# Loading the first batch's Q and K pairs straight into the buffers that TensorE transposes

## The chip, the core and the metric

The kernel runs on one core of one Trainium2 chip. A core has four engines that compute: TensorE (PE in the profile; its weight loads are listed apart, as PEld), VectorE (DVE), ScalarE (ACT) and GpSimd (POOL). SyncE (SP) only issues transfers. Each engine works through its own list of instructions in order, and waits on semaphores for what it needs from the others. Transfers between device memory and the on-chip SBUF go through 16 DMA engines; POOL, SP and ACT can each issue them, and each issuer has a queue of its own. TensorE writes to PSUM, which VectorE and ScalarE read.

The metric is the device time of one execution in microseconds (us), as a median of several runs.

## What is computed

Windowed attention for 8 batches and 8 heads over 576 positions of 64 channels, and behind it a feed-forward layer with squared ReLU on all 4,608 tokens:

```python
# q, k, v: (8, 8, 576, 64) float32
scores = scale * q @ k.transpose(0, 1, 3, 2)           # scale = 1/8
mask = abs(pos[:, None] - pos[None, :]) <= 32
attn = softmax(where(mask, scores, -1e9))
x = (attn @ v).transpose(0, 2, 1, 3).reshape(4608, 512)
h = x @ w_in                                           # (512, 2048)
g = maximum(h, 0) ** 2
out = g @ w_out                                        # (2048, 512), float32
```

## The kernel before

Every batch is cut into three groups of 192 positions; group G is number G mod 3 of batch G div 3, so there are 24 groups. The work of a group, with the names used below and the lines of the profile:

- **Loads** of q, k and v, cast to bfloat16 on the way (POOL). For batches 0 and 1 q and k come as *pairs* (`load_pair`, L426): one partition holds two neighbouring positions of each head, so a written piece is 128 numbers, in the order head, position of the pair, channel. A VectorE copy (L429) then regroups this staging buffer (`PR`, NPR of them for each of q and k) into the buffer `RAW`: all first positions, then all second positions. Group 0 of batch 0 takes another way (`load_hw`, L407): SP loads it in float32, and VectorE and ScalarE cast it into `RAW` (L414, L417). v is loaded in two blocks a group (`load_v`, L443), and VectorE copies the 64 rows that two groups share (`copy_v`, L450).
- **Turn** (`turn_pe`, L485), for batches 0 and 1: TensorE transposes `RAW` in 8 pieces of 128 columns, through the identity matrix, into PSUM; ScalarE (q, L513) or VectorE (k, L516) copies the result to `QT` or `KT`. Later batches are transposed by DMAs that SP issues (L524).
- **S**, the scores (`scores`, L565): two blocks of 8 matmuls, called S1A and S1B for group 1. ScalarE takes the exponential (L589), VectorE multiplies by the mask (L594); for group 0 the mask is added by TensorE ahead of the scores (L548).
- **P** (`pv`, L613 and L622): P0A and P0B for group 0, attention times v. VectorE then takes the reciprocal of the row sums (L641) and normalizes into `xa` or `xb` (L644).
- **T** (`xturn`): the normalized rows are transposed into `XT`, on TensorE for groups 0 to 2 (L666, L671, L696, L701), by DMA later.

The feed-forward layer runs over tokens. **A** is the first product (`mm1`, L737): "A0.12" is tokens from 0 and columns 12 and 13 of the 16 blocks of 128 columns of `w_in`; while a step has 192 tokens, one such item is 8 matmuls. ScalarE applies the ReLU (L743), VectorE squares (L746). **B** is the second product (`mm2`, L757): "B0.2" is the third quarter of the 2,048 terms for output block 0, 4 matmuls.

The weights come in quarters, each one load on POOL's queue: quarter i of `w_in` (L456) is needed first by A0.(4i), and quarter i of `w_out` (L461) by B0.i. In what follows w_in 0 to 3 and w_out 0 to 3 are these quarters.

The order of the work is not written out by hand. Each operation is recorded with its engine, its estimated duration and a key; the method `schedule` plays the program forward with these estimates (those of transfers among them) and gives each engine its fixed list. `OPENING` names the loads at the start in the order of their keys. Where the plan leaves TensorE idle at the start, the program puts in matmuls on a buffer of zeros (L322, "fillers") that compute nothing.

The order of the first loads on POOL's queue is: k1, w_in 0, v0.0, v1.1, q1, v0.1, q2, k2, v1.0, w_in 1, w_in 2, w_in 3, v2.0, v2.1, w_out 1, k3, v3.0, q3, q5, w_out 0, w_out 2, k4, and so on. Here q2 is the load of q for group 2, and v1.0 is block 0 of v for group 1. The sizes written are 192 KB for a pair load of 96 partitions (224 KB for k3, 160 KB for k2 and k5), 512 KB for a weight quarter, and 64 to 128 KB for a block of v.

Of the kernel before, what the change touches and what calls it, by code (L numbers as in the profile page):

```python
# [18 lines left out]
RING = 1536  # L19
NV, NRAW = 6, 6  # L20
NTURN = 2
NXT = 3
LEAD = 13.0
LAG = 9.0
# [9 lines left out]
PMOVE = 20  # L34
# [11 lines left out]
PQ = 100  # L46
VCS = 6
NDUP = 1
NPR = 3
LSLACK1 = 1000  # L50
HOLD = {}
KMIN = 0.5
HOLDT = 26000
KSPL = 0
# [1 line left out]
NSPLIT = 3  # L56
HWB = 150
HWQ = {'k': 'SP', 'q': 'SP'}
HWC = {"k": ("DVE", "ACT"), "q": ("ACT", "DVE")}
NPAIR = 6  # L60
FIRST = {}
T512 = 2048
NBIAS = 1
PKEY = 0.2
MKEY = (-9.5, -6.5)
VSET = (-9.8, -6.8)
ESPLIT = 0
IOTA = -1
OPENING = [("k", 1), ("w1", 0), ("v", 0, 0), ("v", 1, 1), ("q", 1), ("v", 0, 1), ("q", 2), ("k", 2), ("v", 1, 0), ("w1", 1),
           ("w1", 2), ("w1", 3), ("q", 5), ("v", 2, 0), ("v", 2, 1), ("w2", 1), ("k", 3), ("v", 3, 0), ("q", 3), ("w2", 0), ("w2",  # L70
           2), ("k", 4), ("v", 3, 1), ("q", 4), ("v", 5, 0), ("v", 5, 1), ("w2", 3), ("hq", 0), ("k", 5), ("v", 4, 0), ("v", 4, 1),
           ("hk", 0)]
WARM = 40000
LAST = ((0, 256), (256, 384), (384, 512))
KC = ((0, 224), (224, 192), (416, 160))
# [7 lines left out]
class Prog:  # L83
# [43 lines left out]
    def schedule(self):  # L127
# [53 lines left out]
        while True:  # L181
# [21 lines left out]
            first = pool[e][0]  # L203
            soon = min((w[0] for w in wait[e] if t < HOLDT and w[0] <= t + HOLD.get(e, 0) and w[2].key < first[0] - KMIN), default=None)
            if soon is not None and soon - t < first[2].dur:
# [66 lines left out]
def act(n):  # L272
    return 175 + 0.833 * n


def dve(n, fast=True):
    return 153 + (0.52 if fast else 1.04) * n


class Gen:  # L280
# [5 lines left out]
    def alloc(self):  # L286
# [111 lines left out]
    def load_hw(self, t, g, key):  # L398

        t0, n = KC[g] if t == "k" else (192 * g, 192)  # L400
        h = n // 2
        raw = self.RAW[t][g % NRAW]
        u = 2 * (t == "q")
        f = self.OEB[:, u:u + 2, :].rearrange("p a c -> p (a c)")
        s = (self.q if t == "q" else self.k)[0][:, t0:t0 + n, :].rearrange("h (p r) d -> p h (r d)", r=2)
        oe = [("oe", u), ("oe", u + 1)]
        self.p.rec(HWQ[t], lambda e: e.dma_start(f[0:h, :].rearrange("p (h c) -> p h c", c=128), s), writes=oe,  # L407
                   dma=(f"h{u}", g), key=key, dur=420, move=(h // 2, HMOVE), name=f"h{t}{g}")
        for r in range(2):
            x = f[0:h, :].rearrange("p (h r d) -> p h r d", r=2, d=64)[:, :, r, :]  # L410
            y = raw[0:h, r, :].rearrange("p (h d) -> p h d", d=64)
            w = [("raw", t, g % NRAW, r)]
            if HWC[t][r] == "ACT":
                self.p.rec("ACT", lambda e, x=x, y=y: e.activation(y, x, ACTF.Copy), reads=oe, writes=w, key=key, dur=600,  # L414
                           name=f"c{t}{g}{r}")
            else:
                self.p.rec("DVE", lambda e, x=x, y=y: e.tensor_copy(y, x), reads=oe, writes=w, key=key, dur=430, name=f"c{t}{g}{r}")  # L417

    def load_pair(self, t, b, g, key):

        t0, n = KC[g] if t == "k" else (192 * g, 192)
        h = n // 2
        G = 3 * b + g
        pr, raw = self.PR[t][G % NPR], self.RAW[t][G % NRAW]
        s = (self.q if t == "q" else self.k)[b][:, t0:t0 + n, :].rearrange("h (p r) d -> p h (r d)", r=2)
        self.p.rec("POOL", lambda e: e.dma_start(pr[0:h, :].rearrange("p (h c) -> p h c", c=128), s), writes=[("pr", t, G % NPR)],  # L426
                   dma=(f"{t}p{G % NPR}", G), key=key, dur=500 + 3 * h, move=(h // 2, PMOVE), name=f"{t}{b}{g}",
                   slack=LSLACK1 if b else 0)
        self.p.rec("DVE", lambda e: e.tensor_copy(raw[0:h, :, :].rearrange("p r (h d) -> p r h d", d=64),  # L429
                                                  pr[0:h, :].rearrange("p (h r d) -> p r h d", r=2, d=64)),  # L430
                   reads=[("pr", t, G % NPR)], writes=[("raw", t, G % NRAW, x) for x in range(2)], key=3 * G - LEAD - PKEY if b == 0 else key, dur=430,
                   name=f"c{t}{b}{g}")
# [39 lines left out]
    def turn_pe(self, t, b, g, key):  # L472
        dst, n = self.turned(t, b, g)
        h, G = n // 2, 3 * b + g
        raw = self.RAW[t][G % NRAW]
        if b:
            bank, tag = (self.AT[:, 512:1024], self.half(1)) if t == "q" else (self.AT[:, 0:512], self.half(0))
        else:
            bank, tag = (self.OUTP[0][:], ["outp0"]) if t == "k" else (self.HT[1][:], ["ht1"])
        ps = bank.bitcast(BF16)  # L480

        def f(e):
            for j in range(4):
                for x in range(2):
                    mm = e.transpose(ps[:, n * j + h * x:n * j + h * x + h], raw[0:h, x, 128 * j:128 * j + 128],  # L485
                                     self.ID[0:h, 0:h])
            return mm

        self.p.rec("PE", f, reads=[("raw", t, G % NRAW, 0), ("raw", t, G % NRAW, 1), "id"], writes=tag, key=key,
                   dur=8 * 52, name=f"turn{t}{b}{g}")  # L490
        if G < NPAIR:
            src = ps[:, 0:4 * n].rearrange("p (j r q) -> p j r q", j=4, r=2)
            dq = dst.rearrange("p j (q r) -> p j q r", r=2)
            dst = dst.rearrange("p j (q r) -> p j r q", r=2)
            if G < ESPLIT:
                self.p.rec("DVE", lambda e: e.tensor_copy(dst[:, 0:2], src[:, 0:2]), reads=tag, writes=[(t + "h", b % 2, g)],
                           key=key, dur=dve(2 * n, False), name=f"ev{t}{b}{g}h")
                self.p.rec("ACT", lambda e: e.activation(dst[:, 2:4], src[:, 2:4], ACTF.Copy), reads=tag,
                           writes=[(t + "t", b % 2, g)], key=key, dur=act(2 * n), name=f"ev{t}{b}{g}t")
                return  # L500
            dn = dve(4 * n, False)
        else:
            src = ps[:, 0:4 * n].rearrange("p (j q) -> p j q", j=4)
            dn = dve(4 * n)
        w = (t + "t", b % 2, g)
        if t == "k" and G == 0 and KSPL:
            for x, (c0, c1) in enumerate(((0, KSPL), (KSPL, h))):
                self.p.rec("DVE", lambda e, c0=c0, c1=c1: e.tensor_copy(dq[:, :, c0:c1, :].rearrange("p j q r -> p j r q"),
                                                                        src[:, :, :, c0:c1]), reads=tag,
                           writes=[("kt0", x)] if x == 0 else [w], key=key, dur=dve(8 * (c1 - c0), False), name=f"ev{t}{b}{g}{x}")  # L510
            return
        if t == "q":
            self.p.rec("ACT", lambda e: e.activation(dst, src, ACTF.Copy), reads=tag, writes=[w], key=key,  # L513
                       dur=act(4 * n), name=f"ev{t}{b}{g}")
        else:
            self.p.rec("DVE", lambda e: e.tensor_copy(dst, src), reads=tag, writes=[w], key=key, dur=dn,  # L516
                       name=f"ev{t}{b}{g}")
# [16 lines left out]
    def scores(self, G, ws):  # L534
# [35 lines left out]
        if G == 0 and KSPL:  # L570
            rd = [("qt", i, g), ("kt0", 0)] + [("kt", i, 0)] * (1 in ws)
        two = lambda x: b >= NTURN or 3 * b + x < ESPLIT
        rd += [("qh", i, g)] * two(g) + [("kh", i, x) for x in range(max(g - 1, 0), g + 1) if two(x)]
# [78 lines left out]
    def xturn(self, G):  # L652
# [146 lines left out]
    def build(self):  # L799
# [79 lines left out]
    def opening(self):  # L879
        return OPENING  # L880

# [31 lines left out]
```

## Time and profile before

| | |
|---|---|
| median of 3 runs (lowest to highest) | 302.2 us (301.95 to 302.28) |
| the profiled execution | 301.87 us, of which the instructions span 299.9 us |
| PE busy | 291.9 us, 97% of the span |
| VectorE, ScalarE, POOL busy | 167.2, 160.3 and 107.1 us |
| POOL's DMA queue | 106,016 packets, 17.93 MB |

The table is of one profiled execution; its time stands 1.97 us above its span, for what lies around the first and the last instruction. Starts in the trace are microseconds from the start of the span. In a timeline row the columns are: start, time from the first start to the last end, engine, line, operation, what is written and read, sizes, and how many instructions are merged; in brackets stands the idle time of the engine before the row, and what ended it. Matmuls overlap, so the cost of one group on TensorE is the distance from its start to the start of the next one and not the second column.

### The profile page before, as it was taken

The numbers are of one execution on the slowest core, as the hardware profiler recorded it, in microseconds if no ns is written. First come the engines' busy times: TensorE is split into PE (matmuls) and PEld (weight loads), VectorE is DVE, ScalarE is ACT, GpSimd is POOL, SyncE is SP. The second block draws the span as 40 slices with busy tenths as digits, with TensorE's granted clock in tenths as the row PEclk, the third lists the DMA queues.
The fourth block names the chain that finished last, engine by engine and source line by source line (L and its number), as shares of the span: only waits on it lengthen the run. The fifth ranks groups of instructions, "written<-read, shape, count | busy, mean of one in ns | idle before, by whom it ended". The sixth has DMA issues, their size and how long they took to land.

```text
span 299.9 us, 6209 instructions
## 1 busy us (share of the span) xinstructions
PE 291.9 (97%) x2394; PEld 171.8 (57%) x2431; DVE 167.2 (56%) x385; ACT 160.3 (53%) x250; POOL 107.1 (36%) x143
## 2 busy tenths in 40 slices
PE   7899999999999999999999999999999999999996
PEld 3578866848677767664544454444544444444445
DVE  6898775737674767563656666665666632222100
ACT  3497834836467656750765476536744643443312
POOL 8993336503544354455256335533500000000000
PEclk9999999999999999999999999999999999999999
DMA  9999999997999999999999999999992120100112
GB/s 169 176 206 184 196 177 174 169 176 137 164 169 165 95 162 146 155 138 186 180 168 131 114 166 156 125 149 156 154 128 70 55 61 35 37 35 35 38 70 105
DMA packets 160636, 39.83 MB, mean 133 GB/s; under 512 B 149984, under 2 KB 156128, under 8 KB 160608
## 3 DMA queue, kind: packets, MB, share of 16 engines
q0 software_dynamic: 106016, 17.93, 89.3%
q1 hardware_dynamic: 49264, 12.14, 28.5%
q10 hardware_dynamic: 5328, 9.37, 9.1%
q8 instruction: 19, 0.31, 0.5%
q14 instruction: 9, 0.07, 0.1%
HBM read 36.70 MB, written 9.44 MB: 154 GB/s over the span
## 4 chain that ended last, share of the span: by engine, by line
PE 90%; DMA 5%; POOL 3%; issue 1%; ACT 0%; POOLq 0%; ACTq 0%
PE ht L737 41%; PE outp L757 40%; DMA w<-in_moe_w_in_dram 5%; PE at L622 4%; PE at L565 4%; POOL v L443 1%; POOL w L456 1%; PE at L485 1%; PE ht L782 1%; PE outp L782 1%; POOL kpair L426 1%; POOL qpair L426 1%; ACT rt L743 0%; ACT oe L792 0%; POOL dif L325 0%
## 5 line engine op out<-in xcount | busy, mean ns | idle before, releaser
L737 PE MATMUL ht<-xt,w 128*128 128x256 bf16 (+2 forms) x885 | 140.0, 302 | 1.3 <-DMA w<-in_moe_w_in_dram 0.5
L757 PE MATMUL outp<-w,gt 128*128 128x512 bf16 x536 | 133.0, 379 | 1.3
L743 ACT ACTIVATE rt<-ht 128x512 bf16<-128x512 f32 (+1 forms) x152 | 85.9, 578 | 87.1 <-PE ht L737 85.1
L737 PEld LDWEIGHTS ht<-xt,w 128*128 128x128 bf16 x896 | 81.3, 98 | 43.8 <-ACT rt L743 0.6
L746 DVE TENSOR_TENSOR gt<-rt 128x512 bf16<-128x512 bf16 (+1 forms) x152 | 61.5, 408 | 61.6 <-ACT rt L743 60.0
L757 PEld LDWEIGHTS outp<-w,gt 128*128 128x128 bf16 x560 | 51.9, 98 | 54.1 <-ACT oe L767 1.0
L394 POOL DMA_DIRECT2D kraw<-in_k_dram x36 | 27.7, 778 | 107.3 <-PE at L622 56.8
L589 ACT ACTIVATE e<-at 128x1024 bf16<-128x1024 f32 x46 | 44.8, 1021 | 8.7 <-PE at L565 8.4
L594 DVE TENSOR_TENSOR pt<-e,mask 128x1024 bf16<-128x1024 bf16 x46 | 31.8, 691 | 29.0 <-ACT e L589 28.9
L443 POOL DMA_DIRECT2D v<-in_v_dram x48 | 38.2, 809 | 0.0
L767 ACT ACTIVATE oe<-outp 128x512 f32<-128x512 f32 x35 | 21.1, 604 | 29.6 <-PE outp L757 29.6
L394 POOL DMA_DIRECT2D qraw<-in_q_dram x36 | 27.7, 778 | 0.0
L622 PEld LDWEIGHTS at<-v,pt 128*128 128x128 bf16 x384 | 18.3, 98 | 9.9 <-DMA v<-in_v_dram 0.6
L622 PE MATMUL at<-v,pt 128*128 128x65 bf16 x384 | 20.1, 194 | 0.5 <-ACT pt L586 0.5
L644 DVE TENSOR_TENSOR xa<-at,rs 64x512 bf16<-64x512 f32 x24 | 16.7, 695 | 0.9
L644 DVE TENSOR_TENSOR xb<-at,rs 128x512 bf16<-128x512 f32 x24 | 16.5, 689 | 0.7
L565 PEld LDWEIGHTS at<-qt,kt 64*128 64x128 bf16 x384 | 10.8, 94 | 8.7 <-issue 7.1
L565 PE MATMUL at<-qt,kt 64*128 64x128 bf16 x384 | 15.2, 217 | 0.2
L641 DVE RECIPROCAL rs<-at 64x8 f32<-64x8 f32 (+1 forms) x48 | 10.0, 209 | 9.1 <-PE at L622 7.7
L650 DVE MEMSET at<- 64x520 f32 x23 | 11.3, 492 | 3.5 <-DVE xa L644 2.6
L450 DVE COPY v<-v 64x512 bf16<-64x512 bf16 x16 | 5.9, 372 | 5.1 <-PE ht L737 2.9
L789 DVE COPY oe<-ht 128x128 f32<-128x128 f32 x1 | 0.3, 292 | 14.5 <-PE ht L782 14.5
(67 smaller groups left out, 83.2 us busy)
## 6 DMA issues: line engine op xcount, KB each, us to landing
out_dram<-oe ACTq DMA_DIRECT2D x35, 256.0 KB, 3.2
qraw<-in_q_dram POOLq DMA_DIRECT2D x36, 96.0 KB, 5.8
w<-in_moe_w_in_dram POOLq DMA_DIRECT2D x4, 512.0 KB, 10.7
v<-in_v_dram POOLq DMA_DIRECT2D x16, 128.0 KB, 6.6
w<-in_moe_w_out_dram POOLq DMA_DIRECT2D x4, 512.0 KB, 18.8
v<-in_v_dram POOLq DMA_DIRECT2D x16, 96.0 KB, 7.0
kraw<-in_k_dram POOLq DMA_DIRECT2D x12, 112.0 KB, 4.6
kraw<-in_k_dram POOLq DMA_DIRECT2D x12, 96.0 KB, 4.9
```

Source lines behind the costliest of these rows:

```text
L394: self.p.rec("POOL", lambda e, j=j: e.dma_start(raw[0:h, j, :].rearrange("p (h d) -> p h d", h=8), s[:, j]), writes=[("raw", t, G % NRAW, ...
L443: self.p.rec("POOL", lambda e, j=j, lo=lo, hi=hi, k0=k0: e.dma_start(vt[lo - k0:hi - k0, j, :, 0:64], self.v[b, :, lo:hi, :].rearrange("h ...
L565: mm = e.matmul(sc[:, 512 * par + 128 * j:512 * par + 128 * j + 128], kt[r:r + 64, j, k0:k0 + 128], q, start=G >= NBIAS, stop=True, skip_g ...
L589: self.p.rec("ACT", lambda e, e_=e_, sc=sc: e.activation(e_[:], sc, ACTF.Exp, scale=0.125), reads=tags[w], writes=[("e", n % 2)], key=key, ...
L594: self.p.rec("DVE", lambda e, pt=pt, ee=ee, mb=mb: e.tensor_tensor(pt[:], ee, mb, ALU.mult), reads=[("e", n % 2), ("mask", mi)], writes=[( ...
L622: mm = e.matmul(avp[:, c:c + 65], pt[:, 4 * (h % 2) + h // 2, :], vt[:, w, h, 0:65], start=(w == 0 and y == 0), stop=True, skip_group_chec ...
L644: self.p.rec("DVE", lambda e: e.tensor_tensor(x[r0:128, :].rearrange("p (x y c) -> p x y c", x=2, y=4), av[:, :, :, 0:64], rb, ALU.mult), ...
L737: mm = e.matmul(ht[:, n * x:n * x + n], self.W1[:, ft, 128 * d:128 * d + 128], self.XT[:, ft, r:r + n], start=(ft == 0), stop=(ft == 3))
L743: self.p.rec("ACT", lambda e: e.activation(rt[:, 0:c], ht[:, 0:c], ACTF.Relu), reads=[f"ht{k % 2}"], writes=[("rt", k % 4)], key=key, dur= ...
L746: self.p.rec("DVE", lambda e: e.tensor_tensor(gt[:, d0:d0 + len(ds), r:r + n], rr, rr, ALU.mult), reads=[("rt", k % 4)], writes=[("gt", s, ...
L757: mm = e.matmul(op[:], gt[:, d, r:r + 128], self.W2[:, d, :], start=(d == 0), stop=(d == 15))
L767: self.p.rec("ACT", lambda e: e.activation(oe, op[:], ACTF.Copy), reads=[f"outp{u % 2}"], writes=[("oe", u % 4)], key=key, dur=act(512), n ...
```

## The change

Loads of pairs for groups 1 and 2 of batch 0 go straight into `RAW`, in the pair order, and the regrouping copy falls away; the staging buffers are used from group 3 on. The two casts of group 0 write the same pair order. The turn of groups 0 to 2 then takes 64 columns at a time, and sends the two heads of a pair of heads to the lower and the upper 64 partitions of PSUM, so that the result in PSUM is what it was: 16 transposes instead of 8. Some settings of the planner change with it, and the first loads are ordered anew.

```diff
+NRAWP = 3
+TCOL = 200
...
-NPR = 3
+NPR = 4
...
-HOLD = {}
+HOLD = {'PE': 300}
...
-VSET = (-9.8, -6.8)
+VSET = (-12, -9)
...
-OPENING = [("k", 1), ("w1", 0), ("v", 0, 0), ("v", 1, 1), ("q", 1), ("v", 0, 1), ("q", 2), ("k", 2), ("v", 1, 0), ("w1", 1),
...
+OPENING = [("q", 2), ("v", 0, 1), ("v", 0, 0), ("k", 1), ("v", 1, 0), ("q", 1), ("w1", 0), ("hq", 0), ("k", 2), ("w1", 1), ("v",
+           1, 1), ("w1", 2), ("w1", 3), ("v", 2, 0), ("v", 2, 1), ("w2", 0), ("q", 3), ("hk", 0), ("k", 4), ("k", 3), ("v", 5, 0),
+           ("w2", 1), ("v", 4, 1), ("w2", 2), ("v", 3, 0), ("q", 4), ("v", 4, 0), ("v", 3, 1), ("w2", 3), ("v", 5, 1), ("k", 5),
+           ("q", 5)]
...
-            y = raw[0:h, r, :].rearrange("p (h d) -> p h d", d=64)
+            y = self.pairs(raw)[0:h].rearrange("p (h r d) -> p h r d", r=2, d=64)[:, :, r, :]
...
+    def pairs(self, raw):
+        return raw[:].rearrange("p a c -> p (a c)")
+
...
+        if G < NRAWP:
+            self.p.rec("POOL", lambda e: e.dma_start(self.pairs(raw)[0:h].rearrange("p (h c) -> p h c", c=128), s),
+                       writes=[("raw", t, G % NRAW, x) for x in range(2)], dma=(f"{t}P{G}", G), key=key, dur=500 + 3 * h,
+                       move=(h // 2, PMOVE), name=f"{t}{b}{g}")
+            return
...
-                    mm = e.transpose(ps[:, n * j + h * x:n * j + h * x + h], raw[0:h, x, 128 * j:128 * j + 128],
-                                     self.ID[0:h, 0:h])
+                    c = n * j + h * x
+                    if G < NRAWP:
+                        for u in range(2):
+                            d = 256 * j + 128 * u + 64 * x
+                            mm = e.transpose(ps[64 * u:64 * u + 64, c:c + h], self.pairs(raw)[0:h, d:d + 64], self.ID[0:h, 0:h])
+                        continue
+                    mm = e.transpose(ps[:, c:c + h], raw[0:h, x, 128 * j:128 * j + 128], self.ID[0:h, 0:h])
...
-                   dur=8 * 52, name=f"turn{t}{b}{g}")
+                   dur=8 * 52 + TCOL * (G < NRAWP), name=f"turn{t}{b}{g}")
```

In `OPENING`, "w1" is w_in, "w2" is w_out, and "hq" and "hk" are the loads of group 0. `TCOL` is the planner's estimate in ns of what the 16 pieces add to a turn. `HOLD` lets the planner keep an engine waiting up to 300 ns for an operation with a lower key. `VSET` moves two small settings of v's buffers on VectorE. `NPR` is the number of staging buffers.

The order on POOL's queue becomes: q2, v0.1, v0.0, k1, v1.0, q1, w_in 0, k2, w_in 1, v1.1, w_in 2, w_in 3, v2.0, v2.1, w_out 0, q3, k4, k3, v5.0, w_out 1, v4.1, w_out 2, v3.0, q4, v4.0, v3.1, w_out 3, v5.1, k5, q5. The two loads on SP's queue stay first there.

More of the change, by code (lines that the diff above doesn't have):

```diff
@@ L58 @@
 HWQ = {'k': 'SP', 'q': 'SP'}
-HWC = {"k": ("DVE", "ACT"), "q": ("ACT", "DVE")}
+HWC = {'k': ('DVE', 'ACT'), 'q': ('ACT', 'DVE')}
 NPAIR = 6
@@ L65 @@
 MKEY = (-9.5, -6.5)
-VSET = (-9.8, -6.8)
+VSET = (-12, -9)
 ESPLIT = 0
 IOTA = -1
-OPENING = [("k", 1), ("w1", 0), ("v", 0, 0), ("v", 1, 1), ("q", 1), ("v", 0, 1), ("q", 2), ("k", 2), ("v", 1, 0), ("w1", 1),
-           ("w1", 2), ("w1", 3), ("q", 5), ("v", 2, 0), ("v", 2, 1), ("w2", 1), ("k", 3), ("v", 3, 0), ("q", 3), ("w2", 0), ("w2",
-           2), ("k", 4), ("v", 3, 1), ("q", 4), ("v", 5, 0), ("v", 5, 1), ("w2", 3), ("hq", 0), ("k", 5), ("v", 4, 0), ("v", 4, 1),
-           ("hk", 0)]
+OPENING = [("q", 2), ("v", 0, 1), ("v", 0, 0), ("k", 1), ("v", 1, 0), ("q", 1), ("w1", 0), ("hq", 0), ("k", 2), ("w1", 1), ("v",
+           1, 1), ("w1", 2), ("w1", 3), ("v", 2, 0), ("v", 2, 1), ("w2", 0), ("q", 3), ("hk", 0), ("k", 4), ("k", 3), ("v", 5, 0),
+           ("w2", 1), ("v", 4, 1), ("w2", 2), ("v", 3, 0), ("q", 4), ("v", 4, 0), ("v", 3, 1), ("w2", 3), ("v", 5, 1), ("k", 5),
+           ("q", 5)]
 WARM = 40000
```

## The prediction

> **What bounds the kernel now.** I read the page first, then TensorE's waits, then the chain of waits and the first 41 us of the timeline.
>
> ```profile
> span 299.9 us, 6209 instructions
> PE 291.9 (97%) x2394; PEld 171.8 (57%) x2431; DVE 167.2 (56%) x385; ACT 160.3 (53%) x250; POOL 107.1 (36%) x143
> ```
>
> TensorE is busy for 97% of the span, so time can only come from what it waits for, or from fillers at the start, which count as busy. TensorE's waits from 24.2 us (by its matmuls) to the end:
>
> ```profile
> PE ht L737 <- DMA w<-in_moe_w_in_dram: 0.5, 1, 0.5
> PE ht L737 <- ACT rt L743: 0.2, 1, 0.2
> PE ht L737 <- issue: 0.2, 1, 0.2
> ```
>
> The columns are total us, times and longest. The first is the wait that ends at 24.11; behind it come 0.4 us in 276. So the time is the moment 24.11 plus the work left behind it. The chain of waits and the issues name what sets that moment:
>
> ```profile
> 8.72 1.47 POOL w L456 x2
> 10.19 13.79 DMA w<-in_moe_w_in_dram
> ...
> 8.71 2.26 POOL L456 DMA_DIRECT2D w<-in_moe_w_in_dram  x3
> 16.41 1.53 POOL L461 DMA_DIRECT2D w<-in_moe_w_out_dram  x2
> ```
>
> The last quarter of w_in (w_in 3) is issued at 10.19 and has landed at 10.19 + 13.79 = 23.98. A0.12, which needs it, starts at 24.11 and stood idle 0.47 us for it:
>
> ```profile
> 11.18 0.41 PE L622 MATMUL at<-v,pt 128*128 128x65 bf16 x8 [0.54 <-ACT pt L586]
> ...
> 13.78 0.51 PE L485 MATMUL ht<-ident,qraw 96*128 96x96 bf16 x8 [0.17 <-DVE qraw L429]
> 14.13 0.42 PE L613 MATMUL at<-v,pt 128*128 128x65 bf16 x8
> 14.48 0.22 PE L617 MATMUL at<-zz 128*64 128x4 bf16 x2
> 14.64 0.43 PE L622 MATMUL at<-v,pt 128*128 128x65 bf16 x8
> ...
> 17.46 0.83 PE L737 MATMUL ht<-xt,w 128*128 128x192 bf16 x8
> ...
> 21.60 1.49 PE L737 MATMUL ht<-xt,w 128*128 128x192 bf16 x16
> ...
> 23.25 0.40 PE L701 MATMUL at<-ident,xb 128*128 128x128 bf16 x4
> 24.11 1.48 PE L737 MATMUL ht<-xt,w 128*128 128x192 bf16 x16 [0.47 <-DMA w<-in_moe_w_in_dram]
> ```
>
> The transfers from 5 to 24 us, in 40 slices:
>
> ```profile
> DMA  9999999999999999999999999999999999999999
> GB/s 230 183 184 204 209 207 207 205 160 153 156 166 182 169 160 163 182 177 180 172 178 202 207 207 209 201 237 194 200 218 203 198 207 207 207 207 185 157 168 189
> ```
>
> The DMA engines are full in every slice. POOL has issued w_in 3 by 10.97, 13 us before it lands: the transfers are late, not their issue. When each quarter lands is its issue plus the last column here (us to landing), for w_in 1 (issue 8.71), w_in 2 (9.46) and w_out 2 (17.2):
>
> ```profile
> w<-in_moe_w_in_dram POOLq DMA_DIRECT2D x1, 512.0 KB, 9.5
> ...
> w<-in_moe_w_in_dram POOLq DMA_DIRECT2D x1, 512.0 KB, 11.8
> ...
> w<-in_moe_w_out_dram POOLq DMA_DIRECT2D x1, 512.0 KB, 19.7
> ```
>
> That is 18.2, 21.3 and 36.9 us.
>
> **The gate, after the change.** w_in 3 is the twelfth load on POOL's queue before and after. The eleven ahead are the same, in another order: k1, q1, k2, q2, v0.0, v0.1, v1.0, v1.1 and w_in 0, 1, 2; with w_in 3 that is 3,200 KB. A pair load writes the same pieces into another buffer. The two loads on SP's queue stay first there. With full DMA engines the order inside the set does not move its end: 23.98 again, A0.12 at 24.11. What TensorE has done before A0.12 is the same set too by the order that the changed kernel builds: S and P of groups 0 and 1, S2, T0, T1, the six turns, and A0.0 to A0.10. So the work left at 24.11 is unchanged, and whatever the start gains turns into a longer wait for w_in 3, as long as TensorE is there in time.
>
> **The start.** VectorE before:
>
> ```profile
> 8.02 0.42 DVE L429 COPY kraw<-kpair 96x1024 bf16<-96x1024 bf16 x1
> 8.36 1.15 DVE L516 COPY kt<-outp 128x896 bf16<-128x896 bf16 x1
> ...
> 11.72 0.21 DVE L641 RECIPROCAL rs<-at 64x8 f32<-64x8 f32 x1
> 11.97 0.58 DVE L450 COPY v<-v 64x512 bf16<-64x512 bf16 x1
> 12.58 0.69 DVE L644 TENSOR_TENSOR xa<-at,rs 64x512 bf16<-64x512 f32 x1
> 13.30 0.42 DVE L429 COPY qraw<-qpair 96x1024 bf16<-96x1024 bf16 x1
> ```
>
> Four regrouping copies go; the row at 13.30 is the one that counts, for turn q1 waits for it (13.78) and P0B (14.13) stands behind turn q1 on TensorE. The new list also moves the copy at 11.97 behind the normalization, so that ends at 11.93 + 0.69 = 12.6. Turn q1 now stands ahead of that moment, if q1 is there: 864 KB of the 3,200 are issued up to q1, the other 2,336 take 13.2 us at the pace of w_in 2 and 3 (1,024 KB in 23.98 - 18.2 = 5.8 us, 177 KB/us), so q1 lands near 24.0 - 13.2 = 10.8, ahead of P0A (11.18). Were it late, P0B, T0a and S1A would stand behind it on TensorE, and a landing after 12.3 would eat into the gain. P0B moves from 14.13 to about 12.65, a gain of 1.5 us.
>
> From P0B to A0.0 it took 17.46 - 14.13 = 3.33 us. New in between are T0a (0.22), P1A (0.26) and what two dearer turns add. The work itself costs, from start to next start in these rows:
>
> ```profile
> 30.98 0.39 PE L701 MATMUL at<-ident,xb 128*128 128x128 bf16 x4
> 31.20 0.56 PE L485 MATMUL at<-ident,kraw 112*128 112x112 bf16 x8
> 31.60 0.82 PE L737 MATMUL ht<-xt,w 128*128 128x192 bf16 x8
> 32.26 0.51 PE L485 MATMUL at<-ident,qraw 96*128 96x96 bf16 x8
> 32.60 1.49 PE L737 MATMUL ht<-xt,w 128*128 128x192 bf16 x16
> 34.02 0.62 PE L565 MATMUL at<-qt,kt 64*128 64x128 bf16 x16
> 34.57 1.50 PE L737 MATMUL ht<-xt,w 128*128 128x192 bf16 x16
> ...
> 37.89 1.48 PE L737 MATMUL ht<-xt,w 128*128 128x192 bf16 x16
> 39.21 1.03 PE L757 MATMUL outp<-w,gt 128*128 128x512 bf16 x4
> 40.07 0.42 PE L622 MATMUL at<-v,pt 128*128 128x65 bf16 x8
> 40.33 1.48 PE L737 MATMUL ht<-xt,w 128*128 128x192 bf16 x16
> ```
>
> So T half 0.22, turn k 0.40, turn q 0.34, A 0.66 (half of 1.32), S 0.55, B 0.86, P 0.26. A turn of 16 pieces of 64 columns has no row. From below: 16 score matmuls, each on half of the array, take 0.55, so +0.2 a turn. From above: the two 64-column matmuls at 14.48 take 0.16, or 0.08 each, 1.28 for 16, so +0.94. I take +0.2: the scores are the nearer row, with the same count and a split array.
>
> [...]
>
> A0.0 then starts at 12.65 + 3.33 + 0.22 + 0.26 + 0.4 = 16.9, not 17.46. From A0.0 to the end of T1 it took 23.64 - 17.46 = 6.18 (24.11 less the 0.47 idle), with P1A inside, so 5.9 now: TensorE is ready for A0.12 at 22.8. By the other bound, A0.8 waits for w_in 2 (21.3), and A0.8, T1 and A0.10 (0.66 + 0.44 + 0.66) end at 23.1. Either way it is 0.9 us or more ahead of w_in 3. The gain of the start is worth **0**; its price, were that cover gone, is the 24.11 - 23.1 = 1.0 us it could then give.
>
> **Behind the gate** the loads are reordered, and B starts earlier. w_out 0, 1, 2 could be the next to be late. From w_in 3 to w_out 2 it was 2,400 KB (v2.0, v2.1, w_out 1, k3, v3.0, q3, q5, w_out 0, w_out 2) in 36.9 - 24.0 = 12.9 us, 186 KB/us. Now 672 KB lie behind w_in 3 up to w_out 0, 1,856 up to w_out 1, 2,496 up to w_out 2: landing at 27.6, 34.0 and 37.4. TensorE's new order asks:
> - B0.0 after six A and two P: 24.11 + 3.96 + 0.52 = 28.6.
> - B0.1 after B0.0, T2, turns q3 and k3, five A, B1.0: 28.6 + 0.86 + 0.44 + 0.74 + 3.3 + 0.86 = 34.8.
> - B0.2 after B0.1, S3, two A: 34.8 + 0.86 + 0.55 + 1.32 = 37.5.
>
> None waits, the last by 0.1 us only. Term: 0; bounds 0 and, with w_out 1 and 2 as slow as w_in 2 was (21.3 - 18.2 = 3.1 each, not 512 / 186 = 2.75) and no margin, +0.7.
>
> The other settings cost nothing I can find: a fourth staging buffer only lets q5 be issued without waiting for a free one, and the two memsets that `VSET` moves fit into VectorE's idle time before 8.0 us. VectorE's list has the regrouping of q3, k4 and k3 between squares of tokens 192 on; k3 is the last of them, 1,280 KB behind w_in 3, so at 30.9, and the squares queued behind it feed B1.2 and later only, beyond 38.
>
> **The sum**, against the profiled execution (301.87 us, its span of 299.9 and 1.97 around it): gate 0, start 0, w_out 0, so 301.9; the median of the runs stands 0.3 higher, at 302.2, and I forecast **302.2**.
>
> **Rivals.**
>
> *The transfers run faster.* For it: the GB/s row has 207 in the stretches of weights, and w_in 2 took 3.1 us against 2.7 of w_in 3, so size is not all. If 1,024 KB went at 207 GB/s (5.1 us, not 5.8), w_in 3 would land 0.7 earlier, and TensorE is ready for that: **301.5**. Against: all slices full, the same bytes. [...]
>
> *A new wait for w_out 2.* It decides from a landing at 37.5. For it: the margin of 0.1 us. Price up to 0.7: **302.9**, slower than before. Against: TensorE will also lose some tenths on the way, which makes it ask later.
>
> *The turns cost the upper bound.* Turn k0 is on the path to S0: its end was covered by 0.3 us (the copy at 8.02 kept L516 until 8.36), so +0.6 there, and +0.74 more for each of q2 and k2: A0.0 at 16.9 + 2.1 = 19.0, ready at 24.9, 0.8 past the gate: **303.0**. It decides from about +0.6 a turn.
>
> **How the numbers follow.** Forecast 0.54, faster transfers 0.24, w_out 2 0.14, turns 0.08. Within 0.2% (0.6 us, about what a measurement of this kernel tells from no change) lies the forecast: same 0.54, faster 0.24, slower 0.22. The range, 301.3 to 303.0, takes in 0.2 beyond the faster case and ends at the dearest one.
>
> **What would show it.** Right: A0.0 near 16.9, a wait of about 1 us on w_in ahead of A0.12 at 24.1, B0.2 near 37.5. Wrong: w_in 3 landing at another time than 24.0; a TensorE wait on w_out near 37.5; turns of group 0 to 2 over 0.9 us from start to start; the 24.1 being kept while the end moves, which would mean a wait in later batches that this working does not see.

## The result, and the profile after

| | before | after |
|---|---|---|
| median (lowest to highest) | 302.09 us (301.66 to 302.75), 18 runs | 302.62 us (302.05 to 303.27), 18 runs |
| span of the profiled execution | 299.9 us | 300.5 us |

The ratio is 1.0016, with a 95% interval of 1.0009 to 1.0023: slower by 0.5 us, where 302.2 was forecast. The page of the changed kernel, to be held against the first fence of the prediction:

```profile
span 300.5 us, 6284 instructions
PE 291.0 (97%) x2431; PEld 170.5 (57%) x2469; DVE 164.8 (55%) x381; ACT 160.6 (53%) x250; POOL 106.9 (36%) x143
```

TensorE's waits from 24.2 us to the end (total us, times, longest):

```profile
PE ht L752 <- DMA w<-in_moe_w_in_dram: 0.9, 1, 0.9
PE outp L772 <- issue: 0.2, 1, 0.2
PE ht L752 <- issue: 0.2, 1, 0.2
```

The longest wait is the forecast one: 0.9 us for w_in 3, and 0.4 us in all behind it, as before. The chain of waits has the transfer (start, duration):

```profile
10.08 14.15 DMA w<-in_moe_w_in_dram
```

It landed at 10.08 + 14.15 = 24.23; before it was 23.98. TensorE's timeline, from turn q1 to A0.12 and at the two B items that were to be watched:

```profile
11.51 0.53 PE L499 MATMUL ht<-ident,qraw 96*64 96x96 bf16 x16
11.97 0.43 PE L628 MATMUL at<-v,pt 128*128 128x65 bf16 x8
...
13.49 0.53 PE L499 MATMUL ht<-ident,qraw 96*64 96x96 bf16 x16
13.96 0.29 PE L681 MATMUL ht<-ident,xb 128*128 128x128 bf16 x2
...
15.01 0.48 PE L499 MATMUL outp<-ident,kraw 80*64 80x80 bf16 x16
15.50 0.41 PE L637 MATMUL at<-v,pt 128*128 128x65 bf16 x8
15.75 0.82 PE L752 MATMUL ht<-xt,w 128*128 128x192 bf16 x8
...
20.17 0.41 PE L637 MATMUL at<-v,pt 128*128 128x65 bf16 x8 [0.97 <-DVE at L665]
21.44 0.82 PE L752 MATMUL ht<-xt,w 128*128 128x192 bf16 x8 [0.19 <-DMA w<-in_moe_w_in_dram]
22.65 0.82 PE L752 MATMUL ht<-xt,w 128*128 128x192 bf16 x8
24.36 0.82 PE L752 MATMUL ht<-xt,w 128*128 128x192 bf16 x8 [0.89 <-DMA w<-in_moe_w_in_dram]
...
35.57 0.81 PE L772 MATMUL outp<-w,gt 128*128 128x512 bf16 x3
38.20 1.89 PE L772 MATMUL outp<-w,gt 128*128 128x512 bf16 x8
```

Of B0.1's four matmuls the trace has three; the first weight loads of B0.1 and B0.2 are at 35.28 and 38.12.

A turn of 16 pieces takes 0.46 to 0.49 us from its start to the next one (11.51 to 11.97, 13.49 to 13.96, 15.01 to 15.50). A0.0 starts at 15.75, 1.7 us earlier than before. All of that is handed back: 0.97 us at P1B, which waits for VectorE's memset of a PSUM buffer (L665), 0.19 at w_in 2, 0.89 at w_in 3, where it waited 0.47 before. A0.12 starts at 24.36, 0.25 later than before.

### The profile page after: what moved, and what is told of

The parts are those of the page before. It is cut to its first block, busy times and chain, and to the rows that moved or that the text cites. A ratio compares the mean times of both kernels' runs of the same rounds, so it can differ in the third digit from the quotient of the medians.

```text
span 300.5 us, 6284 instructions
## 1 busy us (share of the span) xinstructions
PE 291.0 (97%) x2431; PEld 170.5 (57%) x2469; DVE 164.8 (55%) x381; ACT 160.6 (53%) x250; POOL 106.9 (36%) x143
## 4 chain that ended last, share of the span: by engine, by line
PE 90%; DMA 5%; POOL 3%; issue 1%; ACT 0%; POOLq 0%
PE ht L752 41%; PE outp L772 40%; DMA w<-in_moe_w_in_dram 5%; PE at L580 4%; PE at L637 4%; POOL v L453 1%; POOL w L466 1%; PE at L501 1%; PE ht L797 1%; PE outp L797 1%; POOL qraw L432 1%; POOL kraw L432 0%; ACT rt L758 0%; ACT oe L782 0%; ACT oe L807 0%
## 5 line engine op out<-in xcount | busy, mean ns | idle before, releaser
L396 POOL DMA_DIRECT2D kraw<-in_k_dram x36 | 27.7, 778 | 108.0 <-issue 43.6
L782 ACT ACTIVATE oe<-outp 128x512 f32<-128x512 f32 x35 | 20.9, 599 | 36.1 <-PE outp L772 36.1
L580 PEld LDWEIGHTS at<-qt,kt 64*128 64x128 bf16 x384 | 10.8, 94 | 9.4 <-issue 5.9
L665 DVE MEMSET at<- 64x520 f32 x23 | 11.3, 492 | 3.6 <-DVE xa L659 2.7
```

The costliest lines, as they stand in the source:

```text
L396: self.p.rec("POOL", lambda e, j=j: e.dma_start(raw[0:h, j, :].rearrange("p (h d) -> p h d", h=8), s[:, j]), writes=[("raw", t, G % NRAW, ...
L580: mm = e.matmul(sc[:, 512 * par + 128 * j:512 * par + 128 * j + 128], kt[r:r + 64, j, k0:k0 + 128], q, start=G >= NBIAS, stop=True, skip_g ...
L782: self.p.rec("ACT", lambda e: e.activation(oe, op[:], ACTF.Copy), reads=[f"outp{u % 2}"], writes=[("oe", u % 4)], key=key, dur=act(512), n ...
```

## Experiments

Each set of runs below had runs of the kernel before on the same chip; its median there was 301.98 to 302.14 us. Ratios are against these.

**First set: the change's two halves.** Theory 1 was that the new order of the loads makes w_in 3 late; theory 2 that the 80 to 100 additional instructions of TensorE bring one of its instruction transfers (16,384 bytes; one begins at 27.74 us in the first profile of the kernel before, at 21.56 in that of the changed kernel) ahead of w_in 3; theory 3 that the difference is scatter. r1_before and r1_after are the two kernels. e1_direct has the direct loads and the turns of 16 pieces, with the settings and the order of loads of before; e2_order the reverse:

```diff
 e1_direct, against the changed kernel
-NPR = 4
+NPR = 3
...
-HOLD = {'PE': 300}
+HOLD = {}
...
-VSET = (-12, -9)
+VSET = (-9.8, -6.8)
...
-OPENING = [("q", 2), ("v", 0, 1), ("v", 0, 0), ("k", 1), ("v", 1, 0), ("q", 1), ("w1", 0), ("hq", 0), ("k", 2), ("w1", 1), ("v",
+OPENING = [("k", 1), ("w1", 0), ("v", 0, 0), ("v", 1, 1), ("q", 1), ("v", 0, 1), ("q", 2), ("k", 2), ("v", 1, 0), ("w1", 1),
...
 e2_order, against the changed kernel
-NRAWP = 3
+NRAWP = 0
...
-            y = self.pairs(raw)[0:h].rearrange("p (h r d) -> p h r d", r=2, d=64)[:, :, r, :]
+            y = raw[0:h, r, :].rearrange("p (h d) -> p h d", d=64)
```

> The kernel before, once more, for a second profile. If the moment at which w_in 3 lands is set by the load queue (theory 1 and 2 below), it is within 0.15 us of 23.98 again and A0.12 starts near 24.1. If it scatters by 0.4 us from one execution to the next (theory 3), the later landing in the first profile of the changed kernel explains nothing.

> The changed kernel, once more. Theories 1 and 2: w_in 3 lands at 24.2 to 24.4 again, A0.12 starts 0.25 to 0.4 us later than in the kernel before, and the time is 0.4 to 0.6 us longer. Theory 3: the landing is anywhere from 23.9 to 24.5 and the time is longer all the same.

> Direct loads and 16-piece turns alone: loads in the order of the kernel before, 3 staging buffers, no holding. Theory 1 (the new order of loads delays w_in 3): w_in 3 lands at 24.0, and the time is that of the kernel before within 0.2 us. Theory 2 (the 80 to 100 additional TensorE instructions bring the second fetch of 16 KB of instructions ahead of w_in 3, and the DMA engine that carries it is 0.9 us busy with it): w_in 3 lands 0.2 to 0.4 us late, A0.12 likewise, and the time is 0.2 to 0.5 us longer.

> The new order of loads, 4 staging buffers and the other settings alone: pairs go through the staging buffers and VectorE's regrouping copies, turns in 8 pieces. Theory 1: w_in 3 lands at 24.2 to 24.4 and the time is 0.3 to 0.6 us longer than before. Theory 2: the second fetch of instructions falls behind w_in 3, which lands at 24.0, and the time is that of the kernel before within 0.2 us, if TensorE reaches A0.12 in time with the copies back on VectorE.

| | median us | ratio (95%) | last landing of w_in 3 |
|---|---|---|---|
| r1_before | 302.24 | 1.0008 (0.9999 to 1.0016) | 23.79 |
| r1_after | 304.39 | 1.0073 (1.0057 to 1.0089) | 24.50 |
| e1_direct | 303.29 | 1.0046 (1.0029 to 1.0062) | 24.08 |
| e2_order | 303.57 | 1.0050 (1.0038 to 1.0062) | 24.25 |

The landings of e1_direct and e2_order fit theory 1 by a little, but neither time lies where either theory put it: both are over 1 us above r1_before.

The surprise is r1_after: the same kernel, 1.8 us slower than in its first runs (all 18 of which lay below 303.3). A later w_in 3 can account for 0.3 of it (A0.12 at 24.64, not 24.36). TensorE's timeline there has a wait that the first profile has not:

```profile
24.64 0.82 PE L752 MATMUL ht<-xt,w 128*128 128x192 bf16 x8 [1.23 <-DMA w<-in_moe_w_in_dram]
...
50.59 1.69 PE L772 MATMUL outp<-w,gt 128*128 128x512 bf16 x7 [1.62 <-ACT oe L782]
```

B3.0 writes the PSUM buffer `outp1`, which ScalarE has to copy out first (o1, L782). ScalarE's timeline in r1_after says why that copy is late:

```profile
46.64 0.59 ACT L782 ACTIVATE oe<-outp 128x512 f32<-128x512 f32 x1
47.26 2.63 ACTq L784 DMA_DIRECT2D out_dram<-oe  x1
49.94 0.60 ACT L782 ACTIVATE oe<-outp 128x512 f32<-128x512 f32 x1 [2.71 <-PE outp L772]
...
50.57 0.34 ACTq L784 DMA_DIRECT2D out_dram<-oe  x1
```

The row at 46.64 is o0, the copy of the first output block. The first output store (st0, L784) kept ScalarE's queue for 2.63 us, the second (st1) for 0.34. The wait in brackets is put down to TensorE, whose last products of that block ended at 45.78 + 1.67 = 47.45 by their row, 2.4 us before st0 did (47.26 + 2.63 = 49.89): o1 stood behind st0 on the same engine. In the first profile of the changed kernel the same rows are harmless:

```profile
46.99 0.69 ACTq L784 DMA_DIRECT2D out_dram<-oe  x1
47.73 0.60 ACT L782 ACTIVATE oe<-outp 128x512 f32<-128x512 f32 x1 [0.77 <-PE outp L772]
```

e2_order shows it too, with another item behind the store. There st0 takes 2.00 us, the copy of a turn's result behind it is late, and the scores of group 4 wait 1.37 us (ScalarE, then TensorE):

```profile
45.25 2.00 ACTq L784 DMA_DIRECT2D out_dram<-oe  x1
47.29 1.02 ACT L528 ACTIVATE qt<-at 128x768 bf16<-128x768 bf16 x1 [2.07 <-PE outp L772]
```

```profile
48.37 0.62 PE L580 MATMUL at<-qt,kt 64*128 64x128 bf16 x16 [1.37 <-ACT qt L528]
```

In the first profile of the kernel before, ScalarE has pauses of 1.05 and 0.70 us just ahead, and st0 takes 0.38:

```profile
43.39 1.03 ACT L513 ACTIVATE qt<-at 128x768 bf16<-128x768 bf16 x1 [1.05 <-PE at L485]
45.12 0.60 ACT L767 ACTIVATE oe<-outp 128x512 f32<-128x512 f32 x1 [0.70 <-PE outp L757]
...
45.74 0.38 ACTq L769 DMA_DIRECT2D out_dram<-oe  x1
```

In every one of these profiles the trace has one transfer of 8,192 bytes in an instruction queue near this place: it begins at 43.5 us here, 43.0 in r1_before and 42.7 in e1_direct, over 2 us ahead of st0, but at 46.0 in the first profile of the changed kernel, 45.6 in e2_order and 47.9 in r1_after. From there to the end of st0 it is 1.7 us in the first two of these and 2.0 in r1_after. That made a new theory (A below).

e2_order is 1.33 us above r1_before, about its wait of 1.37. e1_direct loses its 1.05 us elsewhere, only partly located: 0.38 at w_out 3, which it reaches too early,

```profile
44.16 1.90 PE L772 MATMUL outp<-w,gt 128*128 128x512 bf16 x8 [0.38 <-DMA w<-in_moe_w_out_dram]
```

and smaller waits ahead of w_in 1 and 2. So neither half alone is a gain.

**Second set: ScalarE's instruction transfer, the gate, TensorE's transfer.** e3_actpad puts eight tiny copies ahead of ScalarE's list, so that an instruction transfer comes eight instructions earlier; e6_fill gives TensorE other work while it waits for w_in 3 (A192.0 and A192.2 go ahead of A0.12 and A0.14); e4_fetch adds some 100 instructions to TensorE in the kernel before:

```diff
 e3_actpad, against the changed kernel
+        first = min(o.start for o in out if o.eng == "ACT")
+        for k in range(NPAD):
+            w = Op()
+            w.eng, w.fn, w.dma, w.deps, w.i = "ACT", self.pad(k), None, {self.idle_on}, -1
+            w.inc, w.val, w.sem, w.start, w.end, w.dur, w.key = False, None, None, first - 1, 0, 60, -99
...
+        self.p.pad = lambda k: lambda e: e.activation(tiny[:, 4 * k:4 * k + 4], self.ZZ[:, 0:4], ACTF.Copy)
...
 e6_fill, against the changed kernel
-                key = t0 / 64 + d / 16 * n / 64
+                key = t0 / 64 + d / 16 * n / 64 + FILL * (t0 == 0 and d >= 12)
...
 e4_fetch, against the kernel before
-        self.p.idle = lambda e: e.matmul(self.OUTP[1][:], self.ZZ[:, 0:128], self.ZZ[:], start=True, stop=True)
+        def idle(e):
+            for x in range(NFILL):
+                c = 512 // NFILL * x
+                mm = e.matmul(self.OUTP[1][:, c:c + 512 // NFILL], self.ZZ[:, 0:128], self.ZZ[:, 0:512 // NFILL], start=True, stop=True)
+            return mm
+
+        self.p.idle = idle
```

> The changed kernel again, for comparison on this chip. Its two runs so far gave 302.6 and 304.4 us on two chips. Theory A (ScalarE's first output store meets an instruction fetch): the store's issue takes between 0.7 and 2.6 us where every later one takes 0.34 to 0.37, and the time goes with it: about 302.6 us with the short stall, about 304.4 with the long one, in which B3.0 near 50 us waits 1 to 2 us for ScalarE's copy of outp. Theory B (the kernel has two levels by chip, with the first store a bystander): the time lies at 302.6 or 304.4 whatever the first store takes.

> The changed kernel with eight ScalarE copies of 128x4 elements added ahead of ScalarE's first instruction, in a time in which it waits; nothing else differs. Theory A (the 8,192-byte instruction transfer near 46 us is ScalarE's, due at its 68th to 70th instruction, which is its first store): the transfer comes eight instructions earlier, between 40 and 43 us, where ScalarE waits 1.0 to 1.4 us between two copies anyhow; the first store takes 0.34 to 0.40 us, B3.0 doesn't wait for ScalarE, and the time is 0.2 to 0.5 us below the changed kernel on this chip if that shows the short stall, 1.3 to 2.0 below it if it shows the long one. Rival (the transfer belongs to another engine, or the store is held by SyncE's two transposing DMAs that are issued beside it): the transfer stays at 45.5 to 47.8 us, the first store stays over 0.6 us, and the time stays within 0.3 us of the changed kernel's.

> The changed kernel with A0.12 and A0.14 put behind A192.0 and A192.2 in TensorE's list, so that the wait for w_in 3 is filled with work that doesn't need it. If the moment at which w_in 3 lands sets everything behind it: TensorE's wait of 0.9 to 1.2 us ahead of A0.12 shrinks to 0.0 to 0.3 us, and the time falls by 0.5 to 0.9 us against the changed kernel. If the time behind the gate is set by other things (ScalarE's first store, small waits), the wait goes and the time falls by less than 0.3 us.

> The kernel before with each filler matmul of 512 columns replaced by three of 170, which adds about 100 instructions to TensorE ahead of 13 us and no work to speak of; the loads and their order are those of the kernel before. Theory 2 (the second 16,384-byte fetch of TensorE's instructions, brought ahead of w_in 3, delays it): that fetch comes at 20 to 23 us instead of 25 to 28, w_in 3 lands 0.2 to 0.4 us later (24.1 to 24.4 by its last engine) and the time grows by 0.1 to 0.4 us. Theory 1 (the order of the loads delays it): w_in 3 lands at 23.8 to 24.0 as before, and the time is within 0.15 us of the kernel before.

| | median us | ratio (95%) | 8,192-byte transfer at | st0 takes |
|---|---|---|---|---|
| r2_after | 302.50 | 1.0018 (1.0009 to 1.0028) | 45.7 | 0.62 |
| e3_actpad | 303.15 | 1.0034 (1.0022 to 1.0046) | 41.1 | 0.41 |
| e6_fill | 302.52 | 1.0011 (1.0002 to 1.0019) | 45.4 | 0.84 |
| e4_fetch | 302.82 | 1.0036 (1.0019 to 1.0053) | 42.9 | 0.37 |

The transfer moved as theory A has it, and the store went to 0.41 us; so the transfer is ScalarE's. The time was a miss: this chip shows the short stall, nothing was there to be won, and the 0.65 us that e3_actpad is above r2_after (5 runs) are not explained. In e6_fill the long wait for w_in 3 is gone (0.24 us ahead of A192.0, for ScalarE's copy of `XT`), yet the median is that of r2_after (the ratios differ by 0.2 us, and their intervals leave room for nothing and for 0.6): of its two forecasts that is the one in which other things set the time. e4_fetch speaks for theory 2 in part. TensorE's transfer came at 23.2 and w_in 3 landed at 24.25, where theory 2 had 24.1 to 24.4 and theory 1 had 23.8 to 24.0. The time, 0.8 us above the kernel before, can't be used: the cut fillers delay TensorE itself (A0.0 at 18.2, not 17.5), so that it stood idle for w_in 3 no more.

**Third set: the stall, where it is long.** e8_spstore lets SyncE issue st0, all other lists as they were; e7_both is e3_actpad and e6_fill together:

```diff
 e8_spstore, against the changed kernel
-            self.p.rec("ACT", lambda e: e.dma_start(self.out[128 * u:128 * u + 128, :], oe),
+            self.p.rec("SP" if u == 0 else "ACT", lambda e: e.dma_start(self.out[128 * u:128 * u + 128, :], oe),
```

> The changed kernel again, for comparison on this chip: 302.3 to 302.8 us if ScalarE's first output store takes 0.6 to 0.9 us here, some 304.4 us if it takes 2 to 2.6 us and B3.0 then waits for ScalarE.

> The changed kernel with the first output store alone issued by SyncE instead of ScalarE; TensorE's and VectorE's lists stay as they are. If the stall is ScalarE's instruction fetch, the 8,192-byte transfer still comes at about the same instruction of ScalarE (45 to 48 us) and the stall, where this chip shows one, moves to the next instruction of ScalarE (the copy o1 or the exponential X4A starts late by 0.3 to 2 us with its semaphores long there); the store on SyncE takes about as long as others there. If the stall belongs to issuing a first store (a queue that is used for the first time), it goes with the store to SyncE, and ScalarE runs o0, o1, X4A without a gap. Either way the time stays within 0.3 us of the changed kernel if that shows a short stall.

> The changed kernel with A0.12 and A0.14 behind A192.0 and A192.2 and with eight ScalarE copies of 128x4 elements ahead of its first instruction: the wait for w_in 3 filled and the instruction transfer moved off the first store. TensorE waits under 0.3 us ahead of A192.0, the first store takes 0.34 to 0.45 us, and B3.0 doesn't wait. If the gate at w_in 3 is half of what the change lost, the time falls by 0.2 to 0.6 us against the changed kernel, to within 0.2 us of the kernel before; if the gate costs nothing in the end, it stays within 0.15 us of the changed kernel.

| | median us | ratio (95%) | B3.0 waits for o1 |
|---|---|---|---|
| r3_after | 304.33 | 1.0083 (1.0069 to 1.0098) | 1.43 us |
| e8_spstore | 302.72 | 1.0025 (1.0015 to 1.0035) | no |
| e7_both | 302.50 | 1.0021 (1.0010 to 1.0032) | no |

ScalarE in r3_after, and the moved bytes of 47 to 49 us in 40 slices of 0.05 us with the instruction queue's row (transfers, MB, share): the eleventh slice, 47.50 to 47.55, holds the 8,192 bytes.

```profile
47.04 2.44 ACTq L784 DMA_DIRECT2D out_dram<-oe  x1
49.53 0.60 ACT L782 ACTIVATE oe<-outp 128x512 f32<-128x512 f32 x1 [2.52 <-PE outp L772]
```

```profile
GB/s 151 156 146 139 141 149 136 141 154 154 318 151 136 146 138 146 141 149 141 144 156 164 151 154 156 151 146 159 156 161 148 166 161 161 182 179 190 200 210 218
...
q14 instruction: 1, 0.01, 1.3%
```

In e7_both the row of the same queue stands in 40 to 42 us, and st0 is short:

```profile
q14 instruction: 1, 0.01, 1.0%
```

```profile
47.08 0.39 ACTq L795 DMA_DIRECT2D out_dram<-oe  x1
47.52 0.60 ACT L793 ACTIVATE oe<-outp 128x512 f32<-128x512 f32 x1 [0.47 <-PE outp L783]
```

e8_spstore tells the two causes of a stall apart. st0 on SyncE takes 0.38 us, and the transfer still comes at 47.7; now the next store, st1, is held on ScalarE for 1.35 us, up to 49.43 (SyncE, then ScalarE):

```profile
47.22 0.38 SPq L784 DMA_DIRECT2D out_dram<-oe  x1
```

```profile
47.45 0.60 ACT L782 ACTIVATE oe<-outp 128x512 f32<-128x512 f32 x1 [0.26 <-PE outp L772]
48.01 1.02 ACT L604 ACTIVATE e<-at 128x1024 bf16<-128x1024 f32 x1
48.08 1.35 ACTq L784 DMA_DIRECT2D out_dram<-oe  x1
48.93 1.02 ACT L604 ACTIVATE e<-at 128x1024 bf16<-128x1024 f32 x1
```

st1 is the first store of ScalarE there; that it isn't the first use of its queue that costs is seen in e7_both, e3_actpad and the kernel before, where that first use took 0.37 to 0.41 us. In the eight profiles in which ScalarE issued a DMA around such a transfer, the issue ended 1.7 to 2.0 us after the transfer began; the transfer itself took 0.3 to 0.6 us of that, and what the rest is the traces don't tell. The stall moved to st1 and not, as forecast, to o1 or the exponential (X4A, the row at 48.01). The two exponentials stand ahead of st1 in ScalarE's list, so nothing that TensorE needs was late. Both kernels without the stall on o1 are 1.6 and 1.8 us faster than r3_after on the same chip, against a wait of 1.43. The other half of e7_both brought nothing that can be seen: forecast was a time within 0.2 us of the kernel before if the gate is half of the loss, and it is 0.36 above that and level with the changed kernel where its stall is short (302.50 in r2_after).

**Fourth run: more work for the gate.** v 2 lands some 0.5 us behind w_in 3, and P2A waited for it in e7_both (second row):

```profile
23.89 0.83 PE L763 MATMUL ht<-xt,w 128*128 128x192 bf16 x8 [0.24 <-ACT xt L739]
25.09 0.43 PE L648 MATMUL at<-v,pt 128*128 128x65 bf16 x8 [0.36 <-DMA v<-in_v_dram]
```

e9_late puts P2A behind A192.2 as well:

```diff
 e9_late, against e7_both
-        self.p.rec("PE", f, reads=rd + (lo if w and G >= NDUP else []), writes=hi + lo, key=key, dur=260 + 160 * (w and G < NCLR) + 260 * (w and G < NDUP),
+        self.p.rec("PE", f, reads=rd + (lo if w and G >= NDUP else []), writes=hi + lo, key=key + PLATE * (n == 4), dur=260 + 160 * (w and G < NCLR) + 260 * (w and G < NDUP),
```

> As e7_both, with P2A (which needs v 2, the load that lands 0.5 us behind w_in 3) put behind A192.2 in TensorE's list, so that TensorE has work that needs neither w_in 3 nor v 2 until both have landed. If the waits at the gate are half of what the changed kernel lost: no wait over 0.25 us between 22 and 30 us, and 302.0 to 302.3 us, level with the kernel before. If the gate costs nothing in the end, or a wait in a later batch takes its place: 302.4 to 302.8 us, and the profile shows where.

302.52 us (ratio 1.0019, 1.0008 to 1.0030): the first case didn't come. TensorE had no wait over 0.25 us from 22 to 43 us, then 0.21 for w_out 3, which it now reached first:

```profile
23.76 1.49 PE L764 MATMUL ht<-xt,w 128*128 128x192 bf16 x16 [0.24 <-ACT xt L740]
43.54 1.90 PE L784 MATMUL outp<-w,gt 128*128 128x512 bf16 x8 [0.21 <-DMA w<-in_moe_w_out_dram]
```

Three kernels that fill the wait for w_in 3 took 302.50 to 302.52 us, and none is faster than the changed kernel with its short stall. The waits came back in part at other places: from 15.5 to 30 us TensorE's add up to 2.3 us in the first profile of the changed kernel, 2.3 in e7_both, 1.7 in e6_fill and 1.6 in e9_late.

**Last set: does a later gate reach the end?** e10_gate changes the kernel before at one place: v 2.0 and v 2.1 are issued ahead of w_in 3. (They are 160 KB by their issues, not the 192 of the forecast.)

```diff
 e10_gate, against the kernel before
+        w, x, y = (self.named[n] for n in ("w13", "v020", "v021"))
+        w.start, x.start, y.start = y.start, w.start, x.start
```

> The kernel before, a third profile: A0.12 at 23.9 to 24.1, B30.0 at 272.1 to 272.7.

> The changed kernel, a fifth profile: A0.12 at 24.1 to 24.6; B30.0 at 272.8 if the first store of ScalarE is short, 274.6 to 275.0 if it takes over 2 us.

> The kernel before with v 2.0 and v 2.1 (192 KB) put ahead of w_in 3 on POOL's queue; every other list is as it was. 192 KB at the 186 KB/us of the stretch behind w_in 3 make it land 1.0 us later, near 25.0, and A0.12 starts near 25.1. If the moment of A0.12 passes through to the end: 302.9 to 303.2 us, 0.8 to 1.1 above the kernel before. If a later wait absorbs it: 302.1 to 302.6, and the profile has A768.0 at its time of before, 67.4 to 68.2.

e10_gate took 302.98 us, ratio 1.0029 (1.0019 to 1.0039), 0.9 us above the kernel before in the same set. The chain's row for w_in 3 and TensorE's for A0.12, in r4_before:

```profile
10.07 13.87 DMA w<-in_moe_w_in_dram
```

```profile
23.99 1.49 PE L737 MATMUL ht<-xt,w 128*128 128x192 bf16 x16 [0.51 <-DMA w<-in_moe_w_in_dram]
```

and in e10_gate:

```profile
11.62 13.62 DMA w<-in_moe_w_in_dram
```

```profile
25.38 1.48 PE L739 MATMUL ht<-xt,w 128*128 128x192 bf16 x16 [1.63 <-DMA w<-in_moe_w_in_dram]
```

A0.12 is 1.4 us later, the time 0.9 (0.6 to 1.2): a later gate passes through for the most part. r4_after took 304.0 us in its one run, with a first store of 2.51 us and 1.50 us of wait at B3.0; its B30.0 came at 274.19, ahead of the forecast 274.6 to 275.0.

By B30.0 all kernels have done the same items, so its start (first weight load, from the start of the span) compares them:

| | A0.12 | B30.0 |
|---|---|---|
| before: first profile, r1, r4 | 24.08, 23.89, 23.99 | 272.08, 272.62, 272.10 |
| after, the stall not reaching TensorE: first profile, r2, e8_spstore | 24.33, 24.09, 24.58 | 272.64, 272.79, 272.83 |
| e3_actpad, likewise | 24.14 | 272.82 |
| after, the stall reaching TensorE: r1, r3, r4 | 24.60, 24.39, 24.19 | 274.74, 275.03, 274.19 |
| e6_fill, e7_both, e9_late | | 272.30, 272.69, 272.73 |
| e10_gate | 25.34 | 273.35 |

Where the stall doesn't reach TensorE, the changed kernel is 0.35 us later at A0.12 and 0.49 later at B30.0, in the means of three profiles each. But within one kernel the two don't go together: r1_before has the earliest A0.12 of its row and the latest B30.0, and the profiles of after agree at B30.0 within 0.2 though A0.12 differs by 0.5. e6_fill's early B30.0 is that of an execution of 302.19 us, where its median is 302.52. r2_after, early at A0.12, waits again at A768.0, which the trace puts down to nothing ("issue"),

```profile
69.41 1.03 PE L752 MATMUL ht<-xt,w 128*128 128x256 bf16 x8 [0.36 <-issue]
```

and r3_after names what that item waits for, the DMA transposes of the normalized rows into `XT`:

```profile
71.71 0.49 PE L752 MATMUL ht<-xt,w 128*128 128x256 bf16 x3 [0.77 <-DMA xt<-xa]
```

So there can be a second gate near 69 us, which no part of the prediction had; it shows in these two profiles and, with 0.23 us, in r1_before.

## Why the prediction was wrong, and where it held

*The start: right, and too small.* A0.0 came at 15.75 where 16.9 was worked out. Of the 1.1 us, 0.68 is P0B. It was to follow the normalization of P0A, at 12.65, and started at 11.97, behind turn q1 and ahead of that moment:

```profile
12.03 0.69 DVE L659 TENSOR_TENSOR xa<-at,rs 64x512 bf16<-64x512 f32 x1
```

So P0B did not have the wait that the sum put there. q1 landed at 11.46 and not at 10.8, in time all the same. The other 0.43 us are the stretch from P0B to A0.0 (3.78, not 4.21), in part the turns: one of q takes 0.46 or 0.47 against 0.34 with 8 pieces, that of k2 0.49 against 0.40 for k3, where +0.2 was taken. The third rival (+0.6 a turn) is out: 16 pieces of 64 columns took 0.46 to 0.49 from start to next start.

*The gate swallows it: right.* Ahead of A0.12 TensorE was ready at 22.65 + 0.82 = 23.47 and waited 0.89 for w_in 3. "0.9 us or more ahead of w_in 3" was forecast.

*The weights of B: right.* w_out 0, 1 and 2 landed at 27.47, 34.08 and 37.33, within 0.2 us of what was worked out, and B0.1 and B0.2 started at 35.3 and 38.1 with no wait for them, so the second rival didn't come. The margin was 0.8 us and not 0.1, because TensorE asked later than the sum had it. A wait of that kind, for w_out 3, came in e1_direct and e9_late.

*"With full DMA engines the order inside the set does not move its end: 23.98 again, A0.12 at 24.11": the step that failed first.* Its size was 0, and measured is +0.35 to +0.4: A0.12's first weight load is at 23.99 in the mean of three profiles of before, and at 24.36 in the mean of six of after (24.33 in the three whose stall didn't reach TensorE). w_in 3 landing at another time than 24.0 was one of the prediction's own signs of being wrong. The first of the 16 DMA engines ends w_in 3 at 22.5 to 22.7 in both, so the queue's amount was right; the last one ends 1.1 to 1.5 us later in three profiles of before, 1.4 to 2.0 in six of after.

What spreads the engines was not settled. The landings, by the order of the loads and by when TensorE's instruction transfer of 16,384 bytes next came:

| order of loads | transfer at 20.6 to 23.2 us | transfer at 25.2 to 27.7 us |
|---|---|---|
| before | 24.08 (e1), 24.25 (e4) | 23.98, 23.79, 23.95 (first profile, r1, r4) |
| after | 24.23, 24.50, 24.35, 24.14, 24.54 (first profile, r1, r3, r4, e8), 24.03 (e3), 23.76 (e6), 24.22 (e7), 24.12 (e9) | 23.98 (r2), 24.25 (e2) |

With both as in the kernel before, w_in 3 has landed by 23.98 three times out of three. With either one changed it lands at 24.03 to 24.54, but for e6_fill and r2_after. So the step that failed is known and its cause is open: the order, TensorE's transfer, or both.

How much of the 0.5 us it makes up is argued and not shown. For it: 0.35 of the 0.49 us at B30.0 are there at A0.12 already, and in e10_gate a later gate went on to the end. Against it: filling the wait, in e6_fill, e7_both and e9_late, did not bring the time back. The second gate is a candidate for what takes its place, and was not tried.

*"Behind the gate": the step that failed second.* "A wait in later batches that this working does not see" was named as what would make the prediction wrong, and its term was 0 because only transfers and VectorE's list were gone through. ScalarE's list was not. In the new order o1 stands right behind st0, and ScalarE comes to st0 without a pause (r1_after: o0 from 46.64, st0 at 47.26); before, it stood idle for 1.05 and 0.70 us ahead of the two items in front of st0, and the instruction transfer began 2.2 us ahead of st0, longer than the 1.7 to 2.0 us that were measured from a transfer's start to the end of a held issue. In three of five profiles of the changed kernel the stall reached TensorE, with 1.4 to 1.6 us, and these belong to the sets of 304.0 to 304.4. That is shown by e7_both and e8_spstore, which keep it from TensorE by two means. It has no part in the 0.5 us of the first result, in whose profile TensorE has no such wait. Not shown is why the transfer begins 1.0 to 1.1 us ahead of st0 in two profiles of the changed kernel and 0.5 to 0.7 behind its start in three; each set ran on another chip, so whether the chip decides is open too.

*The first rival* (faster transfers, an earlier w_in 3) didn't come in any profile of the changed kernel.

## What to carry to other kernels

A start that gets faster ahead of a late transfer was worth nothing here, and the transfer's *last* engine set the moment: it landed at 23.98 and A0.12's first weight load came at 24.08 in the first profile of the kernel before, 24.23 and 24.33 in that of the changed kernel. What moved that moment by more than its scatter was the amount of bytes ahead of it: in e10_gate, with 160 KB more of them, A0.12 came at 25.34 and not at 23.99 (r4_before). That other work in a wait of 0.9 us gained nothing is a reason to add up all waits of a stretch, and not only the longest. When an order is planned anew, go through every engine's list behind the gate, the idle ones too: ask which instruction now stands behind a DMA issue on the same engine, and who waits for it. A kernel with two levels of time from one set of runs to the next is worth a profile of each level before the cause is looked for in the change.

## What the hardware showed

ScalarE's instructions came in transfers of 8,192 bytes (e3_actpad moved one from 45.7 to 41.1 us with eight instructions), and a DMA issue that met one took longer: 0.62 to 1.35 us where the transfer was under way already, 2.0 to 2.6 us where it began beside the issue, against 0.34 to 0.41 otherwise. All slices of the DMA engines were full at the time, with 2,250 packets of POOL's queue and 155 of another from 47 to 49 us in r3_after. A transfer cost nothing where the next DMA issue of ScalarE came 1.8 us or more behind its start (e10_gate, 0.37 us for st0; before, 2.2 us and 0.38), and 1.4 to 1.6 us of TensorE where it began beside st0 and o1 stood behind (r1_after, r3_after, r4_after). Eight copies of 128x4 elements ahead of ScalarE's first instruction were enough to move it (e3_actpad, st0 0.41 us).
